# An attention and expert kernel: routing products moved to the ends of pairs, column sums moved into another bank, first loads reordered, weight splits brought forward

## The chip, the core and the metric

The kernel runs on one core of a Trainium2 chip. The metric is the device time of one execution in microseconds (us). The core's engines run side by side, each with an instruction stream in program order, and wait for each other by semaphores: TensorE (PE in the profile; PEld is its weight load), VectorE (DVE), ScalarE (ACT), GpSimd (POOL) and SyncE (SP, which mainly issues DMA). PSUM is the memory that TensorE writes to, in eight banks; SBUF is the other on-chip memory.

## What is computed

Three layers follow each other: an attention with positive random features for 2 x 8 heads of 576 tokens, a mixture of 8 experts with a capacity in token order, and a dense layer with a maximum of three products.

```python
def phi(x):                                   # x scaled by 64 ** -0.25
    h = einsum('bhsd,md->bhsm', x, omega) - sum(x * x, -1, keepdims=True) / 2
    return exp(h - max(h, -1)) / sqrt(128)
kv = einsum('bhsm,bhsd->bhmd', phi(k), v);  z = sum(phi(k), axis=2)
x = einsum('bhsm,bhmd->bhsd', phi(q), kv) / (einsum('bhsm,bhm->bhs', phi(q), z) + 1e-6)
x = x.transpose(0, 2, 1, 3).reshape(1152, 512)
expert = argmax(x @ w_gate, 1);  gate = softmax weight of that expert
# token order: expert e takes its first 288 tokens, the rest give zero rows
y[i] = gate[i] * (relu(x[i] @ w1[expert]) @ w2[expert])
out = maximum(maximum(y @ u1, y @ u2), y @ u3) @ w_out    # 512 -> 768 -> 512
```

## The kernel before

**Attention in pairs.** Two heads make a pair; there are eight, `i` = 0 to 7, four per batch. The main loop stands near the end of the part before the experts. For pair `i` TensorE does `kv_mm` (key features times values, L295, into bank `kb`), `q_t` (transposes of the query features, L328), `z_mm` (column sums of the key features, L308 and L310, into a tile `zq` of the two-bank pool `nb`), `kv_t` (transposed back, L319, into another part of `kb`), `q_th` (the transpose of the last half tile, L333, into `zq`), then for pair `i + 1` the projections (`proj`, L242, and `proj_half`, L264), and last `num(i)` (L342 and L346, into `nb`). VectorE takes a minimum over each projection (`mn`, L249 and L270), ScalarE makes the features with it (`kp` for keys and `qp` for queries, L254 and L274), GpSimd adds the key features up (`ks` and `ksum`, L286 and L288), and VectorE divides what `num` gave (L352 to L369). Projections, transposes and the small tiles of the routing share a pool `pj` of five PSUM banks.

**Routing.** When batch 0's four pairs are done, its routing runs beside pairs 4 to 7 as a generator, `side0`: `route` picks each token's expert (LG to OH), counts tokens per expert with small products `rp` (L456 and L458), chooses the busiest expert, makes a selection matrix `pm` (five 128x288 comparisons, L514) and the tokens' numbers and gates `VAL` (L444 to L450), and gets the row lists from 15 small products `vps` (L529). GpSimd then gathers the rows by DMA (L538) and TensorE transposes them (`tps`, L817) into `xth` and `xtl`. The main loop calls `step()` at fixed places of a pair, and each call takes the generator to its next `yield`; strings such as `YS` and `YP` say where `route` yields. So the program order on every engine is written out by the kernel itself. Batch 1's routing (`side1`) runs the same way beside the first expert's products.

**Experts.** Each pass takes 288 rows through one expert. A float32 product is made of three: operands are split into a rounded part (`hi`, ScalarE, L772) and a rest (`lo`, L773, by GpSimd or VectorE as a letter of `SUBS` says). `pump()` lets `split` take the next weight tile; it may run ahead by `HLB` pairs of buffers. `stage1(0, ...)` (L140 to L142, out of `hps`; eight products, `h1` to `h8` below) begins inside pair 7: three stand before `num(7)`, the others after it. ScalarE takes each out (`hh`, L839) and VectorE forms its rest (`hl`, L840). `stage2` gives `y`. The remaining time is the second expert, a small third job, and the dense layer.

**Loads.** SyncE issues nearly all DMA in program order. The first are omega (`om`, two halves), then pair 0's keys in two parts, its queries, pair 1's, and the values `va`.

Of the kernel before, what the change touches and what calls it, by code (L numbers as in the profile page):

```python
# [8 lines left out]
F32 = mybir.dt.float32  # L9
F32R = mybir.dt.float32r  # L10
BF16 = mybir.dt.bfloat16
# [12 lines left out]
M = 128  # L24
# [11 lines left out]
W1, W2, W3 = 2, 2, 0  # L36
LE, LW = 2, 3
RA, RB, RM = 0, 1, 1
R0, S0, LG1, LV, PMG = 4, 5, 3, (2, 4), ()
# [14 lines left out]
SUBS = "GGGGGGGVVVVVVVVVVVVVVVVVVVVV"  # L54
# [3 lines left out]
YS = "110110011"  # L58
YP = "11000"
LG0, NP0 = 2, 3  # L60
# [6 lines left out]
RAWB, HLB, W64B, EB, CB = 8, 4, 4, 3, 5  # L67

@with_exitstack
def favor_moe_kernel(ctx, tc, qk, va, omt, wg, w1, w2, wm, wo, cap, out):  # L70
# [31 lines left out]
    def load_pair(i):  # L102
        b, p = divmod(i, NP)
        qk_t[i] = ldp.tile([128, 2, 640], F32, tag="qk", name="qk", bufs=2)
        if i == 0:
            SP.dma_start(qk_t[i][:, 0, 0:256], qk[b, p, :, 0, 0:256])
            SP.dma_start(qk_t[i][:, 0, 256:640], qk[b, p, :, 0, 256:640])
            SP.dma_start(qk_t[i][:, 1, :], qk[b, p, :, 1, :])
        else:
            SP.dma_start(qk_t[i], qk[b, p])  # L110
        if i > 1:
            load_va(i)
# [7 lines left out]
    for h in range(2):  # L120
        SP.dma_start(om0[64 * h:64 * h + 64, :], omt[64 * h:64 * h + 64, M * h:M * h + M])
    load_pair(0)

    warm = once.tile([128, 512], BF16, name="warm")
# [4 lines left out]
    for _ in range(WARM):  # L129
        T.matmul(wps, lhsT=warm[:, 128:256], rhs=warm, start=True, stop=True)  # L130
# [101 lines left out]
    KP, QP, QT, KV, KS, MN, ZQ = {}, {}, {}, {}, {}, {}, {}  # L232
# [57 lines left out]
    def kv_mm(i):  # L290

        kb = pk.tile([128, 512], F32, tag="kb", name="kb")
        for t in range(5):
            for h in range(2):
                T.matmul(  # L295
                    kb[64 * h:64 * h + 64, 0:M], lhsT=va_t[i][:, 4 * h + t if t < 4 else 8 + h, :],
                    rhs=KP[i][:, 4 * h + t if t < 4 else 8, :], start=(t == 0), stop=(t == 4),
                    tile_position=(0, 64 * h),
                )
        kvt = kqp.tile([128, M], F32, tag="kvt", name="kvt")  # L300
        copy(KTS[i], kvt, kb[:, 0:M])
        KV[i] = (kb, kvt)

    def z_mm(i):

        ZQ[i] = pn.tile([128, 2, 512], F32, tag="nb", name="zq")
        z = ZQ[i][:, 1, 0:2]
        T.matmul(z, lhsT=KP[i][:, 8], rhs=half, start=True, stop=False)  # L308
        for h in range(2):
            T.matmul(z[:, h:h + 1], lhsT=KS[i][:, h], rhs=one, start=False, stop=(h == 1))  # L310
        kva = kqp.tile([128, 2, VC], F32, tag="kva", name="kva")
        V.tensor_copy(kva[:, :, XC], z)
        KV[i] += (kva,)

    def kv_t(i):

        kb, kvt, kva = KV[i]
        kv = kb[:, 2 * M:2 * M + 2 * XC].rearrange("p (h c) -> p h c", h=2)
        T.matmul(kv, lhsT=kvt, rhs=idw[:, i % NP], start=True, stop=True)  # L319
        copy(KVS[i], kva[:, :, 0:XC], kv)  # L320
        KV[i] = (kb, kva)
# [9 lines left out]
    def q_th(i):  # L331
        ps = ZQ[i][:, 0, 0:128]
        T.transpose(ps, QP[i][:, 8, :], ident)  # L333
        copy(QHS[i], QT[i][:, 8, :], ps)
# [78 lines left out]
    def route(b, lag, slow):  # L413
# [20 lines left out]
        for _ in range(lag):  # L434
            yield
        def gates():
# [86 lines left out]
        for _ in range(LV[b]):  # L523
            yield
# [164 lines left out]
    now = [0]  # L689
    stamp = {}  # L690
# [177 lines left out]
    def step(n=1):  # L868
        for _ in range(n):
# [34 lines left out]
    def side0():  # L904
# [5 lines left out]
        for _ in range(W3):  # L910
            yield
# [42 lines left out]
    def a_step():  # L954
        while len(s1) == 8 and fill:
            step()
# [5 lines left out]
    for i in range(NPR):  # L962
# [7 lines left out]
        step()  # L970
        kv_t(i)
        q_th(i)
# [27 lines left out]
        else:  # L1000
# [3 lines left out]
            a_step()  # L1004
        num(i)
        for _ in range(CP.count(i)):
            next(cons)
        step()
# [322 lines left out]
```

## Time and profile before

| | us |
|---|---|
| three runs | 236.82, 239.42, 241.21 (median 239.42) |
| the profiled execution | 239.82 |
| its span in the trace | 237.7 |

| engine | busy us | share of the span | instructions |
|---|---|---|---|
| PE | 221.4 | 93% | 1924 |
| PEld | 202.8 | 85% | 1924 |
| DVE | 143.1 | 60% | 387 |
| ACT | 109.4 | 46% | 268 |
| POOL | 63.2 | 27% | 94 |

The profile is of one execution. Times count from the start of the span. A row of a timeline gives start, duration, engine, line, operation, output and inputs, and in brackets how long the engine stood idle before and what ended that. Equal neighbours are merged (x16 is sixteen instructions, with one duration from the first to the last). Matmul ends are modelled. PEclk is TensorE's granted clock as a share of its upper level.

### The profile page before, as it was taken

Reading aid. Unit: us, or ns where it says so; the run is one execution under the profiler, and the core shown is the slowest. Engines: PE = TensorE matmul, PEld = TensorE weight load, DVE = VectorE, ACT = ScalarE, POOL = GpSimd, SP = SyncE. Lnnn points to the kernel's source line nnn. Section 1 sums busy time; section 2 is a strip of 40 time slices with the busy share of each in tenths; the row PEclk is TensorE's granted clock in tenths of the full one; section 3 lists DMA queues with packets and bytes.
Section 4 is the critical chain, followed back from the end, with each engine's and each line's share of the span. In section 5 each row is a group of like instructions: output and inputs, shape, how many; then the busy total and the mean of one; then the engine's idle time right before and its main releaser. Section 6 shows DMA issues by size and latency. Waiting matters only on the chain. (4 is left out here: it accounts for less than half of the span.)

```text
span 237.7 us, 5117 instructions
## 1 busy us (share of the span) xinstructions
PE 221.4 (93%) x1924; PEld 202.8 (85%) x1924; DVE 143.1 (60%) x387; ACT 109.4 (46%) x268; POOL 63.2 (27%) x94
## 2 busy tenths in 40 slices
PE   7699999998989999879999999999999999999970
PEld 3598998887967999869899989899999999988870
DVE  0665676798866217997898795675964464432120
ACT  2866966782876443410696936544722213100000
POOL 7004523330486094714100000021321101013120
PEclk9999999997997799979999999999999999999997
DMA  4938759996830812855999678976500000001210
GB/s 118 331 85 280 234 166 338 309 309 228 324 99 3 288 61 81 296 211 165 347 403 411 216 246 276 406 257 219 176 1 3 0 0 3 1 1 47 88 47 29
DMA packets 15821, 42.22 MB, mean 178 GB/s; under 512 B 2269, under 2 KB 5213, under 8 KB 15792
## 3 DMA queue, kind: packets, MB, share of 16 engines
q1 hardware_dynamic: 14304, 39.39, 47.4%
q0 software_dynamic: 800, 2.44, 3.1%
q8 instruction: 17, 0.28, 0.5%
q10 hardware_dynamic: 688, 0.02, 0.2%
q14 instruction: 12, 0.10, 0.1%
HBM read 34.36 MB, written 7.54 MB: 176 GB/s over the span
## 5 line engine op out<-in xcount | busy, mean ns | idle before, releaser
L140 PE MATMUL m<-YH,hi 128*128 128x288 f32 (+1 forms) x144 | 43.6, 303 | 0.0
L141 PE MATMUL m<-YL,hi 128*128 128x288 f32 (+1 forms) x144 | 43.0, 299 | 0.0
L142 PE MATMUL m<-YH,lo 128*128 128x288 f32 (+1 forms) x144 | 42.9, 298 | 0.0
L772 ACT CAST hi<-raw 128x1024 fp32r<-128x1024 f32 x28 | 29.3, 1051 | 26.5 <-PE m L141 16.7
L773 DVE TENSOR_TENSOR lo<-raw,hi 128x1024 fp32r<-128x1024 f32 x21 | 25.9, 1232 | 17.3 <-ACT hi L772 15.9
L140 PEld LDWEIGHTS m<-YH,hi 128*128 128x128 f32 x144 | 27.1, 188 | 0.8 <-issue 0.6
L254 ACT ACTIVATE kp<-ps,mn 128x128 f32<-128x128 f32 x64 | 17.4, 383 | 21.1 <-DVE mn L249 21.1
L142 PEld LDWEIGHTS m<-YH,lo 128*128 128x128 f32 x144 | 27.1, 188 | 0.0
L141 PEld LDWEIGHTS m<-YL,hi 128*128 128x128 f32 x144 | 27.1, 188 | 0.0
L249 DVE TENSOR_REDUCE mn<-ps 128x4 f32<-128x512 f32 x32 | 20.5, 683 | 7.1 <-PE ps L242 7.1
L672 ACT CAST e<-w 128x512 f16<-128x512 bf16 x24 | 18.8, 785 | 10.2 <-DMA w<-in_wm_dram 6.8
L140 PE MATMUL y<-hh,hi 128*128 128x288 f32 x64 | 20.4, 318 | 0.8 <-DVE KC L476 0.8
L286 POOL TENSOR_TENSOR ks<-kp 128x512 f32<-128x512 f32 x7 | 9.1, 1298 | 42.4 <-ACT kp L254 42.4
L1160 POOL TENSOR_TENSOR H2L<-mxt,H2H 128x288 fp32r<-128x288 f32 (+1 forms) x10 | 9.5, 948 | 38.7 <-ACT H2H L95 24.9
L242 PE MATMUL ps<-om,qk 64*128 64x128 f32 x256 | 18.7, 300 | 0.9 <-DMA qk<-in_qk_dram 0.9
L141 PE MATMUL y<-hl,hi 128*128 128x288 f32 x64 | 19.5, 305 | 0.0
L142 PE MATMUL y<-hh,lo 128*128 128x288 f32 x64 | 19.5, 305 | 0.0
L242 PEld LDWEIGHTS ps<-om,qk 64*128 64x128 f32 x256 | 17.0, 209 | 2.9 <-DVE om L919 1.1
L773 POOL TENSOR_TENSOR lo<-raw,hi 128x1024 fp32r<-128x1024 f32 x7 | 16.5, 2380 | 10.9 <-ACT hi L772 10.7
L140 PE MATMUL hps<-xth,hi 128*128 128x288 f32 x64 | 19.3, 301 | 0.0
L141 PE MATMUL hps<-xtl,hi 128*128 128x288 f32 x64 | 18.9, 295 | 0.0
L142 PE MATMUL hps<-xth,lo 128*128 128x288 f32 x64 | 18.8, 294 | 0.0
(228 smaller groups left out, 466.8 us busy)
## 6 DMA issues: line engine op xcount, KB each, us to landing
w<-in_wm_dram SPq DMA_DIRECT2D x18, 512.0 KB, 5.5
raw<-in_w_dram SPq DMA_DIRECT2D x16, 512.0 KB, 6.1
qk<-in_qk_dram SPq DMA_DIRECT2D x7, 640.0 KB, 5.5
craw<-in_w_dram SPq DMA_DIRECT2D x8, 512.0 KB, 9.3
w<-in_wo_dram SPq DMA_DIRECT2D x6, 512.0 KB, 5.2
va<-in_va_dram SPq DMA_DIRECT2D x8, 320.0 KB, 5.8
out_dram<-zt SPq DMA_DIRECT2D x9, 256.0 KB, 5.4
XD<-X SPq DMA_DIRECT2D x2, 960.0 KB, 6.3
```

What stands on the lines that cost most here:

```text
L140: T.matmul(ps, lhsT=wh, rhs=xh, start=start, stop=False)
L141: T.matmul(ps, lhsT=wh, rhs=xl, start=False, stop=False)
L142: T.matmul(ps, lhsT=wl, rhs=xh, start=False, stop=stop)
L242: T.matmul(ps[h][:, t, :], lhsT=qk_t[i][r, s, 128 * t:128 * t + 128], rhs=om[r], start=True, stop=True, tile_position=(64 * h, 0),)
L249: V.tensor_reduce(MN[i][:, k:k + 4], PJ[i, s][h], axis=AX.X, op=ALU.min)
L254: A.activation(dst[:, 4 * h + t, :], PJ[i, s][h][:, t, :], AF.Exp, bias=mn[:, k + t:k + t + 1], scale=-1.0)
L286: eng.tensor_tensor(u, k4[:, 0:2], k4[:, 2:4], ALU.add)
L672: A.copy(e.bitcast(F16).rearrange("p (c two) -> p c two", two=2)[:, :, 1], src.bitcast(BF16)[:, 4:4 * WH + 4:4])
L772: A.copy(hi, raw)
L773: (G if SUBS[n] == "G" else V).tensor_tensor(lo, raw, hi, ALU.subtract)
L1160: engine(HLS[k]).tensor_tensor(H2L[:, fc, n0:n1], mv, H2H[:, fc, n0:n1], ALU.subtract)
```

## The change

Seven things change.

- `z_mm` writes its sums into the bank `kb`, next to `kv_t`'s output, and `q_th` into the second quarter of that bank; `zq` goes. One VectorE copy then takes values and sums together (`kva`, 128x146), and the separate 128x2 copy goes. `q_th` is issued ahead of `kv_t`.
- A flag `spot` is true in the `step` at a pair's end. `rp`, `vps` and the row transposes of batch 0 wait for it, so they follow `num` (pairs 4, 5 and 6). The yields `YS`, `YP`, `LG0`, `LV`, `W1` to `W3` are set anew.
- The first load on SyncE is now the first part of the keys; omega's halves go one by ScalarE's queue and one as SyncE's second load.
- `HLB` goes from 4 to 6: six pairs of split buffers.
- Ahead of `num(7)` three more `pump()` calls split three more weight tiles.
- `SUBS`: the rests of tiles 4 to 6 are formed by VectorE, not GpSimd.
- The warm-up tile shrinks from 512 to 128 columns, read four times over; `kvt` has one buffer.

```diff
-W1, W2, W3 = 2, 2, 0
+W1, W2 = 2, 1
-R0, S0, LG1, LV, PMG = 4, 5, 3, (2, 4), ()
+R0, S0, LG1, LV, PMG = 4, 5, 3, (0, 4), ()
-SUBS = "GGGGGGGVVVVVVVVVVVVVVVVVVVVV"
+SUBS = "GGGGVVVVVVVVVVVVVVVVVVVVVVVV"
-YS = "110110011"
-YP = "11000"
-LG0, NP0 = 2, 3
+YS = "111100101"
+YP = "01000"
+LG0, NP0 = 0, 3
-RAWB, HLB, W64B, EB, CB = 8, 4, 4, 3, 5
+RAWB, HLB, W64B, EB, CB = 8, 6, 4, 3, 5
@@ load_pair, i == 0
             SP.dma_start(qk_t[i][:, 0, 0:256], qk[b, p, :, 0, 0:256])
+            SP.dma_start(om0[64:128, :], omt[64:128, M:2 * M])
             SP.dma_start(qk_t[i][:, 0, 256:640], qk[b, p, :, 0, 256:640])
@@
-    for h in range(2):
-        SP.dma_start(om0[64 * h:64 * h + 64, :], omt[64 * h:64 * h + 64, M * h:M * h + M])
+    A.dma_start(om0[0:64, :], omt[0:64, 0:M])
     load_pair(0)
-    warm = once.tile([128, 512], BF16, name="warm")
+    warm = once.tile([128, 128], BF16, name="warm")
-        T.matmul(wps, lhsT=warm[:, 128:256], rhs=warm, start=True, stop=True)
+        T.matmul(wps, lhsT=warm, rhs=warm.unsqueeze(1).to_broadcast([128, 4, 128]), start=True, stop=True)
@@ z_mm, kv_t, q_th
-        ZQ[i] = pn.tile([128, 2, 512], F32, tag="nb", name="zq")
-        z = ZQ[i][:, 1, 0:2]
+        kb, kvt = KV[i]
+        z = kb[:, 2 * M:2 * M + 2 * VC].rearrange("p (h c) -> p h c", h=2)[:, :, XC]
...
+        T.matmul(kv[:, :, 0:XC], lhsT=kvt, rhs=idw[:, i % NP], start=True, stop=True)
+        copy(QHS[i], QT[i][:, 8, :], kb[:, M:2 * M])
         kva = kqp.tile([128, 2, VC], F32, tag="kva", name="kva")
-        V.tensor_copy(kva[:, :, XC], z)
...
+        copy(KVS[i], kva, kv)
-        ps = ZQ[i][:, 0, 0:128]
-        T.transpose(ps, QP[i][:, 8, :], ident)
-        copy(QHS[i], QT[i][:, 8, :], ps)
+        T.transpose(KV[i][0][:, M:2 * M], QP[i][:, 8, :], ident)
@@ route, twice: before rp and before vps
+        while slow and not spot[0]:
+            yield
@@ step
-    def step(n=1):
-        for _ in range(n):
+    def step(end=False):
+        spot[0] = end
@@ side0, before the row transposes
-        for _ in range(W3):
+        while not spot[0]:
             yield
@@ main loop
+        q_th(i)
         kv_t(i)
-        q_th(i)
...
+        if not more:
+            for _ in range(3):
+                pump()
         num(i)
         for _ in range(CP.count(i)):
             next(cons)
-        step()
+        step(True)
```

Line numbers in the rows of the changed program below are its own, a few off those of before: its L339 and L343 are `num`, L530 is `vps`, L513 `pm`, L842 `hl`, L775 the rest `lo`.

TensorE's queue in pair 5, before, from the last projection (`psh`) to pair 6's first product (`kb`):

```order
L264 MATMUL psh<-om,qk 64x128 x4
L529 LDWEIGHTS pm
L529 MATMUL vps<-VAL,pm 128x6
...
L342 MATMUL nb<-kva,qt 128x73 x8
L346 MATMUL nb<-kva,qt 64x73 x2
L295 MATMUL kb<-kp,va 64x128 x10
```

The same place in the changed program:

```order
L264 MATMUL psh<-om,qk 64x128 x4
L339 MATMUL nb<-kva,qt 128x73 x8
L343 MATMUL nb<-kva,qt 64x73 x2
L530 LDWEIGHTS pm
L530 MATMUL vps<-VAL,pm 128x6
...
L295 MATMUL kb<-kp,va 64x128 x10
```

`vps`, fifteen loads and products that need all five `pm`, moved from ahead of `num` to behind it; nothing of pair 6 may pass it.

VectorE's queue in the same pair, before, from the selection's start to the first minimum reduction of pair 6's projections (`sm` are small routing tiles, `KC` a count):

```order
L510 SCALAR_TENSOR_TENSOR sm_903<-sm_903,RG 128x5
L446 TENSOR_TENSOR sm_859<-GT,VAL 128x5
L514 TENSOR_SCALAR pm<-io,sm_903 128x288
L448 CAST VAL<-sm_859 128x5
L312 COPY kva<-zq 128x2
L514 TENSOR_SCALAR pm<-io,sm_903 128x288
L450 TENSOR_TENSOR VAL<-sm_859,VAL 128x5
L95 COPY kva<-kb 128x2x72
L95 COPY qt<-zq 128x128
L514 TENSOR_SCALAR pm<-io,sm_903 128x288 x3
L519 COPY KC<-KT 128x8
L249 TENSOR_REDUCE mn<-ps_956 128x4
```

In the changed program, from the first reduction on:

```order
L249 TENSOR_REDUCE mn<-ps_923 128x4
L249 TENSOR_REDUCE mn<-ps_924 128x4
L270 TENSOR_REDUCE mn<-psh 128x2
L249 TENSOR_REDUCE mn<-ps_933 128x4
L249 TENSOR_REDUCE mn<-ps_934 128x4
L509 SCALAR_TENSOR_TENSOR sm_955<-sm_955,RG 128x5
L445 TENSOR_TENSOR sm_880<-GT,VAL 128x5
L513 TENSOR_SCALAR pm<-io,sm_955 128x288
L447 CAST VAL<-sm_880 128x5
L513 TENSOR_SCALAR pm<-io,sm_955 128x288
L449 TENSOR_TENSOR VAL<-sm_880,VAL 128x5
L513 TENSOR_SCALAR pm<-io,sm_955 128x288 x3
```

The selection moved from ahead of the five reductions to behind them.

VectorE's queue around `num(7)`, before, from the rests of `h1` and `h2` to the division:

```order
L840 SCALAR_TENSOR_TENSOR hl<-hps,hh 128x288 x2
L352 TENSOR_SCALAR dn_149<-nb 128x2x4
L353 TENSOR_SCALAR dn_149<-nb 64x2
L354 RECIPROCAL dn_149<-dn_149 128x10
L357 TENSOR_TENSOR X<-nb,dn_149 128x2x4x64
```

And in the changed program:

```order
L842 SCALAR_TENSOR_TENSOR hl<-hps,hh 128x288 x2
L775 TENSOR_TENSOR lo<-raw,hi 128x1024 x3
L349 TENSOR_SCALAR dn_149<-nb 128x2x4
L350 TENSOR_SCALAR dn_149<-nb 64x2
L351 RECIPROCAL dn_149<-dn_149 128x10
```

Three splits moved in ahead of the division; one more (the tile after them) now stands between the rests of `h3` and `h4`, ahead of the second routing's counts, and GpSimd has two splits fewer behind pair 7.

## Rows read from the trace of the kernel before

**Rows 1.** Stretches: width, busy us (instructions) of each engine, PEclk, DMA share, GB/s

```profile
18.26:26.42 8.16, 8.16 (x101) 7.38 (x101) 5.36 (x17) 5.89 (x23) 3.06 (x10) 1.00 0.69 236
...
42.81:52.08 9.27, 8.50 (x108) 7.60 (x108) 7.97 (x28) 6.86 (x27) 2.71 (x3) 1.00 0.98 323
...
52.08:63.70 11.62, 10.64 (x116) 9.52 (x116) 9.59 (x48) 6.58 (x25) 2.43 (x4) 0.85 0.81 303
...
63.70:77.08 13.38, 12.13 (x113) 9.60 (x111) 8.72 (x30) 9.38 (x28) 10.17 (x8) 0.88 0.20 60
...
77.08:81.97 4.89, 4.89 (x39) 4.44 (x38) 0.96 (x3) 2.02 (x5) 0.00 (x0) 0.64 0.81 244
...
86.84:104.06 17.22, 14.69 (x128) 14.07 (x126) 13.22 (x51) 4.98 (x10) 9.21 (x5) 1.00 0.52 177
...
104.06:112.06 8.00, 8.00 (x52) 8.00 (x50) 6.98 (x32) 1.05 (x1) 3.50 (x4) 0.79 0.42 143
...
112.06:230.00 117.94, 117.94 (x919) 111.17 (x918) 70.05 (x130) 47.02 (x76) 15.76 (x17) 1.00 0.44 161
```

**Rows 2.** What TensorE waited for, whole span: us in total, times, longest

```profile
PE kb L295 <- DMA va<-in_va_dram: 1.4, 1, 1.4
...
PE zq L308 <- DVE sm L503: 0.8, 1, 0.8
...
PE y L140 <- DVE KC L476: 0.8, 1, 0.8
```

**Rows 3.** Timeline of TensorE, three places

```profile
21.61 2.06 PE L242 MATMUL ps<-om,qk 64*128 64x128 f32 x32
...
103.53 0.60 PE L529 MATMUL vps<-VAL,pm 128*128 128x6 bf16 x15 [1.75 <-DVE hl L840]
...
116.90 1.10 PE L817 MATMUL tps<-ident,rows 128*128 128x128 f32 x6
```

**Rows 4.** Timeline of SyncE's DMA issues, the start

```profile
0.80 1.21 SPq L121 DMA_DIRECT2D om<-in_omt_dram  x2
...
3.16 0.43 SPq L108 DMA_DIRECT2D qk<-in_qk_dram  x1
```

**Rows 5.** DMA issues: engine, count, KB each, median us from issue to landing

```profile
qk<-in_qk_dram SPq DMA_DIRECT2D x1, 320.0 KB, 3.7
...
rows<-XD,IX POOLq DMA_INDIRECT x6, 3.4
```

**Rows 6.** Timeline of VectorE: an ordinary pair, then the second routing

```profile
21.72 0.29 DVE L95 COPY qt<-zq 128x128 f32<-128x128 f32 x1
...
24.64 1.28 DVE L249 TENSOR_REDUCE mn<-ps 128x4 f32<-128x512 f32 x2
...
89.17 0.17 DVE L352 TENSOR_SCALAR dn<-nb 128x8 f32<-128x8 f32 x1 [2.83 <-PE nb L346]
...
95.21 1.72 DVE L473 TENSOR_TENSOR sm<-TOT,KT 128x8 f32<-128x8 f32 x1
...
100.02 0.15 DVE L399 TENSOR_REDUCE sm<-sm 128x1 f32<-128x8 f32 x1
...
101.28 0.16 DVE L510 SCALAR_TENSOR_TENSOR sm<-sm,RG 128x5 f32<-128x5 f32 x1
...
103.02 1.55 DVE L840 SCALAR_TENSOR_TENSOR hl<-hps,hh 128x288 fp32r<-128x288 f32 x4
```

**Rows 7.** Timeline of GpSimd: an ordinary pair, then the second routing

```profile
25.79 1.30 POOL L286 TENSOR_TENSOR ks<-kp 128x512 f32<-128x512 f32 x1 [4.95 <-ACT kp L254]
...
27.17 0.72 POOL L288 TENSOR_TENSOR ksum<-ks 128x256 f32<-128x256 f32 x1
...
94.50 4.76 POOL L773 TENSOR_TENSOR lo<-raw,hi 128x1024 fp32r<-128x1024 f32 x2 [3.20 <-ACT hi L772]
...
108.26 1.25 POOL L538 DMA_INDIRECT rows<-XD,IX  x1 [0.30 <-issue]
```

**Rows 8.** Costliest groups of the page: count | busy us, mean ns | idle before

```profile
L773 DVE TENSOR_TENSOR lo<-raw,hi 128x1024 fp32r<-128x1024 f32 x21 | 25.9, 1232 | 17.3 <-ACT hi L772 15.9
```

## What the change does to the time: the prediction

> **What bounds the kernel now.** I read it by stages first: the table of busy time by stretch [rows 1], cut at TensorE's own marks. From 112.06 us to 230 us TensorE is busy 117.94 of 117.94 us at full clock, so nothing outside TensorE's own work is to be won there. An ordinary attention pair takes 8.16 us and is full as well. The loss sits between: pair 4 takes 9.27 us, pair 5 11.62, pair 6 13.38; pair 7 needs 4.89 to the first expert product; and the stretch from pair 7's `num` (86.84) to the end of `vps` (104.06) holds 14.69 us of work in 17.22. So whatever the change wins, apart from the start, has to come from about 55 us in the middle.
>
> Second comes the granted clock in the same rows, whose two levels are 1.2 and 2.4 GHz: 0.85, 0.88, 0.64 and 0.79 in four stretches. A mean of 0.85 over 11.62 us is 2 x 0.15 x 11.62 = 3.5 us at the lower level, which costs half of that, 1.7 us; the others work out to 1.6, 1.8 and 1.7. Before them TensorE waited: 0.8 us in pair 5 for a VectorE operation of the routing, at `z_mm` [rows 2], and 1.75 us before `vps` [rows 3]. Third are the waits by line [rows 2] and the timelines of VectorE and GpSimd [rows 6, 7], which say what was late.
>
> **The change part by part**, against the profiled execution's 239.8 us (span 237.7; the shown median is 239.4, so the two stand level).
>
> *Start.* SyncE issued two loads of omega in 1.21 us before the keys, and the queries' half, issued at 3.16, landed 3.7 us later [rows 4, 5], at 6.86, with `va` later still: TensorE waited 1.4 us for it [rows 2]. One omega load now goes by ScalarE's queue, so SyncE's later loads, `va` too, move up by 0.6 us. Omega's second half is still SyncE's second load, so TensorE's first product stays where it is; what follows moves up. I take -0.6; nothing if ScalarE were the limit, -0.8 at most with the smaller warm-up tile. Only the issue slots are counted, not more bandwidth.
>
> *Sums in the values' bank.* `z_mm` no longer takes the `nb` tile, so it doesn't wait for `num`'s readers; one small VectorE copy per pair goes, hidden in idle time. But `z` now waits for ScalarE's copy `kvt`, which reads that bank and stands behind the features. An ordinary pair has little room there; bounds 0 and +0.1 a pair; I take +0.3 for eight.
>
> *Routing products at the ends, pair 4.* `rp` stands behind `num` and no longer waits for a feature buffer, and `z`'s wait goes too. The pair falls to 8.16 plus a few small products, 8.3: -1.0.
>
> *Pair 5*, where a new wait arises. Its seven late selection rows (`far`, `VAL`, five `pm`) stood ahead of the five minimum reductions in VectorE's queue; now they stand behind them, and `vps` follows `num`. From the pair's first product: VectorE's two copies end at 21.72 + 0.29 - 18.26 = 3.75; twelve routing operations take 100.02 to 101.28, 1.26 us [rows 6], so the reductions start at 5.0 and, two pairs of 1.28 [rows 6] and a short one between, some 2.9 in all, end at 7.9. The selection takes 101.28 to 103.02, 1.74: the last `pm` is done at 9.6 and `vps` at 10.0. `num` alone would be through at 8.2, so TensorE stands about 1.3 us, with all of pair 6 queued behind it. That is the bound if GpSimd doesn't interfere. The other bound: GpSimd's key sums, 1.30 and 0.72 us [rows 7], start just then, once the keys' features are out; if the small copies and differences between the `pm` are held until each ends, 1.5 us more: 11.5. I take 10.7, between, since such small operations are the kind held in [rows 6], but the `pm` themselves have no row beside a GpSimd operation. Against 11.62: -0.9.
>
> The lock is in this trace: a 128x8 difference took 1.72 us at 95.21, while GpSimd's splits ran from 94.50 to 99.26 [rows 6, 7]. The Trainium skill (SBUF — State Buffer, "Who interferes with whom") says that a VectorE operation with two SBUF inputs and a GpSimd one that reads SBUF exclude each other for the whole instruction, the first to issue winning; the trace agrees. By that rule alone pair 5 would take 11.5 us, and it speaks against this order.
>
> *Pairs 6 and 7.* They took 13.38 + 4.89 = 18.27, of which 3.4 us went to the lower clock. The work is 8.16, twelve row transposes (six took 1.10 [rows 3], so 2.2), and 21.61 - 18.26 = 3.35 from a pair's first product to its projections, where pair 7 has the expert products instead: 13.7. The gathered rows may arrive up to 0.4 late, since `vps` and the list after it come later. After a stand of over a microsecond in pair 5 I expect one stretch at the lower clock again, 1.7 us, which hides the rows: 15.4, so -2.85. If the clock stays up: 14.1, -4.2. If it falls for as long as before: 17.1, -1.2.
>
> *Stage 1.* GpSimd keeps two splits fewer after `num`, so two operations of the second routing are free: the difference that took 1.72 us, and the limit behind it, held until the split ended at 99.26 [rows 6, 7], together some 4 us. That removes the waits of 0.8 (`y`) [rows 2] and 1.75 (`vps`) [rows 3]. In exchange three splits of 1.23 us each [rows 8] stand on VectorE ahead of `num(7)`'s division. VectorE was idle 2.83 us there [rows 6]; 3 x 1.23, plus about 0.7 in which the first is held by GpSimd's last split of 2.38 us, is 4.4, so the division and all routing behind it start 1.6 later. `rp` then waits about 0.6, the next two expert products 0.9 and 0.5 (the seventh split stands between their two `hl`): 2.0 come, 2.5 go, about -0.6. Afterwards the gather decides: before, its third part was issued at 108.26 [rows 7] and took 3.4 [rows 5], to 111.7, against the transposes at 112.06. Even at full clock these can move up only by what `vps` moved, plus 0.4. I take -0.9 (bounds 0 and -1.4). Six buffers only allow the forward splits; the later splits run two ahead of a TensorE that never waited there.
>
> Sum: -0.6 + 0.3 - 1.0 - 0.9 - 2.85 - 0.9 = -5.95, from 239.8 to **233.9 us**, 2.3% under the median. About 2% (4.8 us) is what a measurement of this kernel can tell from no change, so this stands at 234.6's edge.
>
> **The rivals.**
> - *Clean middle, 231.9.* Nothing holds the `pm` (pair 5 at 10.0: a further -0.7) and the clock stays up through pairs 6 and 7 (a further -1.35), rest as above. For it: TensorE stood 1.4 us at the start [rows 2] and no low clock followed. Against it: each middle wait of 0.8 us or more was followed by a low stretch.
> - *GpSimd's lock in pair 5, 237.3.* The `pm` chain is held by both key sums (11.5: +0.8), the longer stand pulls the clock down for as long as it was low before in pairs 6 and 7 (17.1: +1.65), and stage 1, whose gather waits for the same queue, gives nothing (+0.9). For it: [rows 6], and that all three hang on VectorE's longer queue. The page's rule on the shared port is this rival's first term.
> - *Slower, 245.* The seventh load of expert weights, queued on SyncE behind pair 6's store of `X`, lands late. ScalarE's cast of it stands ahead of the routing's exponential, and VectorE's split of it ahead of `num(7)`. Before, that cast came only after this exponential, so lateness was covered; now every microsecond beyond about 10 us after pair 7's start is one of TensorE's. From 6 us late the total is above the old one; 11 us give 245. Against it: the 320 KB load landed in 3.7 us [rows 5], and no row of the expert loads shows a wait of TensorE.
> - *Not what it says*: the rows move, but the clock falls in the same places whatever the waits. Then only the waits go: -0.6 + 0.3 - 1.0 - 1.2 - 0.6, 236.7; counted with the second rival.
>
> **How the numbers follow.** Forecast 233.9 (232.5 to 235.6): 0.42. Clean, 230 to 232.5: 0.25. Lock or low clock anyway, 235.6 to 238.5: 0.27. Slower: 0.06. The range, 230.3 to 238.0, leaves out the slower rival and the outer ends of the two others, some 0.15 in all. Faster by over 2% (under 234.6): the clean case and two thirds of the forecast, 0.53. Within 2%: 0.41. Slower by over 2%: 0.06.
>
> **What would show it.** Right: pair 5's `vps` waits for a `pm` by 1 to 3 us; pairs 4 and 6 show no wait for a feature buffer; the difference of totals in the second routing takes 0.2 us, not 1.7; VectorE's first forward split takes about 1.9 us beside GpSimd's. Wrong: if pair 5 shows no wait at `vps`, my queue count failed; if granted clock stays 1.00 in pairs 5 to 7 after such a wait, the 1.7 is not owed; if the products after `rp` don't wait, the forward splits cost nothing.

## The result and the profile after

The changed kernel takes 236.07 us (median of 20 executions, 234.17 to 238.35), where the kernel before, run in turn with it, takes 241.12. The ratio is 0.9883, with a 95% interval from 0.9848 to 0.9919. It leaves out executions over 1.5% above the fastest of each kernel (the rest average 238.6 and 235.9), so it is nearer to 1 than the two medians are. The change is a gain of 1.2%; I had forecast 2.3% to 2.5%. The direction was right, and 236.07 lies inside the range, but the gain is half of the forecast.

The profiled execution took 235.41 us with a span of 233.7, against 239.82 and 237.7: 4.0 us less, where my sum said 5.95. The profiled execution of the kernel before thus lies 1.2 us above the average just given, that of the changed kernel 0.4 below its own. The table of busy time by stretch, cut at TensorE's marks as [rows 1] was, shows where they went (columns: stretch and width, then busy us of TensorE, its weight load, VectorE, ScalarE, GpSimd, the granted clock, DMA share, GB/s):

```profile
18.53:42.78 24.25, 24.25 (x295) 22.10 (x295) 15.10 (x44) 17.61 (x65) 9.52 (x32) 1.00 0.80 258
42.78:51.23 8.45, 8.45 (x106) 7.60 (x104) 6.84 (x23) 6.46 (x25) 2.29 (x3) 1.00 0.99 332
51.23:63.09 11.86, 9.29 (x117) 8.18 (x113) 10.68 (x49) 7.60 (x28) 3.34 (x4) 0.91 0.58 213
63.09:74.51 11.42, 11.42 (x107) 10.08 (x104) 6.49 (x25) 7.30 (x21) 8.50 (x6) 0.80 0.47 169
74.51:78.65 4.14, 4.14 (x44) 3.55 (x44) 2.73 (x9) 3.21 (x11) 1.31 (x2) 1.00 0.63 200
78.65:100.07 21.42, 19.75 (x164) 19.01 (x162) 16.62 (x60) 8.75 (x16) 6.16 (x3) 1.00 0.55 178
100.07:106.53 6.46, 6.46 (x51) 6.46 (x49) 5.94 (x31) 2.11 (x2) 3.36 (x4) 1.00 0.70 233
...
106.53:112.82 6.29, 5.95 (x48) 4.88 (x47) 2.98 (x8) 3.30 (x7) 0.12 (x1) 1.00 0.84 291
112.82:126.86 14.04, 13.20 (x96) 12.93 (x97) 13.97 (x24) 11.36 (x21) 0.82 (x1) 1.00 0.96 375
```

The last two, from the first row transposes to the second expert's first product and from there to its first `y`, have these counterparts in the kernel before, which the prediction had not looked at one by one:

```profile
112.06:117.93 5.87, 5.87 (x48) 4.85 (x47) 3.93 (x10) 3.10 (x5) 0.93 (x1) 1.00 0.92 338
117.93:130.83 12.90, 12.90 (x97) 12.90 (x97) 11.88 (x20) 10.17 (x19) 0.00 (x0) 1.00 1.02 406
```

| stretch | before, us | after, us | difference | forecast |
|---|---|---|---|---|
| to the end of pair 0's `num` | 18.26 | 18.53 | +0.27 | -0.6 |
| pairs 1 to 3 | 24.55 | 24.25 | -0.30 | about +0.1 |
| pair 4 | 9.27 | 8.45 | -0.82 | -1.0 |
| pair 5 | 11.62 | 11.86 | +0.24 | -0.9 |
| pairs 6 and 7, to the first expert product | 18.27 | 15.56 | -2.71 | -2.85 |
| to the end of the second `vps` | 22.09 | 21.42 | -0.67 | with the next row |
| to the first row transposes | 8.00 | 6.46 | -1.54 | -0.9 for the two |
| to the second expert's first `y` | 18.77 | 20.33 | +1.56 | 0 |
| from there | 106.87 | 106.84 | -0.03 | 0 |
| sum | 237.7 | 233.7 | -4.0 | -5.95 |

(The bank's +0.3 was spread over eight pairs in the forecast; 0.2 of it has no line of its own.)

The largest difference, -2.71, can't be put down to the change. The low granted clock of the kernel before in pairs 6 and 7 (0.88 and 0.64 in [rows 1]) belongs to its one profiled execution. The run `before_new_loads`, reported below, differs from the kernel before only in its first loads, and its two stretches from pair 6 to the first expert product are at full clock:

```profile
63.67:75.57 11.90, 10.93 (x113) 8.89 (x113) 7.61 (x26) 9.35 (x28) 10.03 (x8) 1.00 0.24 69
75.57:78.81 3.24, 3.24 (x38) 2.96 (x38) 1.74 (x7) 1.91 (x5) 0.00 (x0) 1.00 0.46 172
```

That is 15.14 us instead of 18.27, with the same operations in the same order there. Against it the changed kernel's 15.56 is no gain. The whole span of that run was 234.3, only 0.6 above the changed kernel's. The averages differ by 2.7 us, between this 0.6 and the 4.0 of the two profiles; that would fit if some executions of the kernel before have the low stretch and others don't, but in how many was not counted.

What TensorE waited for (us in total, times, longest), to be held against [rows 2]:

```profile
PE vps L530 <- DVE VAL L449: 2.3, 1, 2.3
PE kb L295 <- DMA va<-in_va_dram: 2.0, 1, 2.0
PE hps L140 <- DVE hl L842: 1.1, 2, 0.9
...
PE hps L141 <- DVE xtl L811: 0.8, 1, 0.8
PE rp L455 <- DVE OH L424: 0.6, 1, 0.6
```

Gone are the waits at `zq` and `y`, and those for the feature buffers. Of these the kernel before had one of 0.5 at `rp` and two at the row transposes:

```profile
PE tps L817 <- ACT kp L254: 1.0, 2, 0.5
```

Three things stand in their place: `vps` of pair 5 (2.3), `rp` and two `hps` in stage 1 (1.7 together), and two `hps` of the second expert (0.3 and 0.8), which no step of mine had (the wait of 0.3 is for `idt`, a small VectorE tile). The timelines show the first. VectorE in pair 5, then GpSimd, then TensorE:

```profile
56.35 1.28 DVE L249 TENSOR_REDUCE mn<-ps 128x4 f32<-128x512 f32 x2
...
59.32 0.37 DVE L513 TENSOR_SCALAR pm<-io,sm 128x288 bf16<-128x288 f32 x1
59.61 1.24 DVE L447 CAST VAL<-sm 128x5 bf16<-128x5 f32 x1
60.75 0.35 DVE L513 TENSOR_SCALAR pm<-io,sm 128x288 bf16<-128x288 f32 x1
61.03 0.69 DVE L449 TENSOR_TENSOR VAL<-sm,VAL 128x5 bf16<-128x5 f32 x1
61.63 0.92 DVE L513 TENSOR_SCALAR pm<-io,sm 128x288 bf16<-128x288 f32 x3
```

```profile
59.44 1.37 POOL L286 TENSOR_TENSOR ks<-kp 128x512 f32<-128x512 f32 x1 [6.97 <-ACT kp L254]
60.89 0.80 POOL L288 TENSOR_TENSOR ksum<-ks 128x256 f32<-128x256 f32 x1
```

```profile
61.78 1.38 PE L530 MATMUL vps<-VAL,pm 128*128 128x6 bf16 x15 [2.33 <-DVE VAL L449]
63.09 2.40 PE L295 MATMUL kb<-kp,va 128*64 128x128 f32 x20
```

The cast ends with GpSimd's `ks` (60.8), the difference with its `ksum` (61.7). In the second routing, with GpSimd idle, the same two take 0.17 us each, so 1.6 us are held. Then `kv_mm`, 1.31 us in other pairs, takes 2.40, at the lower clock (0.80 over pair 6).

### The profile page after: what moved, and what is told of

Same layout as the page of the kernel before. It is cut to its first block, busy times and chain, and to the rows that moved or that the text cites. A ratio compares the mean times of both kernels' runs of the same rounds, so it can differ in the third digit from the quotient of the medians.

```text
span 233.7 us, 5130 instructions
## 1 busy us (share of the span) xinstructions
PE 217.4 (93%) x1924; PEld 199.8 (86%) x1924; DVE 141.8 (61%) x382; ACT 109.7 (47%) x268; POOL 56.1 (24%) x91
## 5 line engine op out<-in xcount | busy, mean ns | idle before, releaser
L775 DVE TENSOR_TENSOR lo<-raw,hi 128x1024 fp32r<-128x1024 f32 x24 | 30.1, 1262 | 15.2 <-ACT hi L774 15.2
L673 ACT CAST e<-w 128x512 f16<-128x512 bf16 x24 | 18.8, 785 | 11.7 <-DMA w<-in_wm_dram 10.6
L140 PE MATMUL y<-hh,hi 128*128 128x288 f32 x64 | 19.6, 306 | 0.0
L677 DVE SCALAR_TENSOR_TENSOR raw<-w,e 128x512 int32<-128x512 int32 x24 | 17.1, 714 | 3.5 <-ACT e L673 3.4
L142 PE MATMUL y<-hh,lo 128*128 128x288 f32 x64 | 18.8, 294 | 0.0
L141 PE MATMUL y<-hl,hi 128*128 128x288 f32 x64 | 18.8, 294 | 0.0
L1163 DVE TENSOR_TENSOR mxt<-m,mxt 128x288 f32<-128x288 f32 (+1 forms) x24 | 11.1, 462 | 12.1 <-PE m L142 11.6
L242 PEld LDWEIGHTS ps<-om,qk 64*128 64x128 f32 x256 | 15.7, 195 | 2.7 <-DVE om L922 1.4
```

What stands on the lines that cost most here:

```text
L140: T.matmul(ps, lhsT=wh, rhs=xh, start=start, stop=False)
L141: T.matmul(ps, lhsT=wh, rhs=xl, start=False, stop=False)
L142: T.matmul(ps, lhsT=wl, rhs=xh, start=False, stop=stop)
L242: T.matmul(ps[h][:, t, :], lhsT=qk_t[i][r, s, 128 * t:128 * t + 128], rhs=om[r], start=True, stop=True, tile_position=(64 * h, 0),)
L673: A.copy(e.bitcast(F16).rearrange("p (c two) -> p c two", two=2)[:, :, 1], src.bitcast(BF16)[:, 4:4 * WH + 4:4])
L677: V.scalar_tensor_tensor(dst.bitcast(I32), src[:, 1:2 * WH + 1:2], 13, e, ALU.logical_shift_right, ALU.bitwise_or)
```

## The experiments

The kernels were measured in four groups, each with the kernel before in it, whose median was 238.3 to 241.2. A ratio is to the kernel before of the same group, so ratios of different groups compare only roughly; mechanisms are held against rows, which are of one execution each.

**Gates ahead of the reductions.** The gates are three small operations that make `VAL` (L445 to L449): a difference, a cast and a difference.

```
+        if slow:
+            for _ in gt:
+                pass
         if slow and YS[8] == "1":
             yield
         V.scalar_tensor_tensor(far, far, BIG, r, ALU.mult, ALU.add)
-        next(gt)
+        next(gt, None)
```

> The changed kernel, with the three small gate operations (a difference, a cast and a difference into VAL) moved ahead of the five minimum reductions in pair 5; the five pm stay behind them. In the changed kernel the cast took 1.24 us and the last difference 0.69 beside GpSimd's key sums, where the second routing's took 0.17 each, so 1.6 us are held. Theory (GpSimd's lock on these two is what turns a short wait into 2.33 us): the two take 0.2 each again, vps waits 0.3 to 0.8 us, and TensorE's granted clock stays at 1.00 behind it (pair 6 in 10.5 or less instead of 11.42): 2.5 to 3.3 us less in all. Rival 1 (the queue is too long by itself, the pm are then held in their stead): vps still waits 1.8 or more, no gain. Rival 2 (the wait goes, but the clock falls at that place whatever the wait): the wait shrinks, pair 6 still shows a low stretch, 1.3 to 1.8 us less.

Ratio 0.9919 (0.9876 to 0.9962). The cast and the last difference took 0.18 us each again, but pair 5 took 12.14 us, not less, and TensorE stood 2.5 us at `vps` in three pieces. VectorE's rows show why; the first is of all five `pm`, the others of the second and the third:

```profile
59.55 3.05 DVE L516 TENSOR_SCALAR pm<-io,sm 128x288 bf16<-128x288 f32 x5
...
59.84 1.40 DVE L516 TENSOR_SCALAR pm<-io,sm 128x288 bf16<-128x288 f32 x1
...
61.17 0.88 DVE L516 TENSOR_SCALAR pm<-io,sm 128x288 bf16<-128x288 f32 x1
```

The five `pm` take 3.05 us instead of 1.5. The first starts just ahead of GpSimd's sums (59.68) and takes its usual 0.37 us. The second takes 1.40 and the third 0.88; they end just after GpSimd's `ks` (61.08) and `ksum` (61.87). Rival 1 held: whatever stands at that place is held, the `pm` too. My prediction had left open whether the `pm` are of that kind.

**GpSimd's sums after the `pm`.** This takes the overlap away and leaves VectorE's order as it is.

```
+    PMS = []
...
+        PMS.append(pm)
...
-            sums(nx)
+            if nx != 6:
+                sums(nx)
...
             step()
             step()
+            if nx == 6:
+                G.tensor_copy(sm([128, 1]), PMS[0][:, NT - 1, 0:1])
+                sums(nx)
```

> The changed kernel; GpSimd's key sums for pair 6 are issued in pair 5 only when the fifth pm is out (one 128x1 copy of it on GpSimd ahead of them), the order on VectorE stays. In the run with the gates first, the five pm took 3.05 us beside those sums where five unheld ones take 1.5, so what stands there is held, whatever it is. Theory (GpSimd's lock is about half of the wait, the queue the other half): the cast and the difference take 0.2 each, the wait at vps falls from 2.33 to 0.7 to 1.2 us, the first pair-6 product comes about 10.2 to 10.6 us after pair 5's (11.86 before), and z_mm(6) doesn't wait for the later sums. If a wait of about 1 us is still followed by a lower clock, pair 6 keeps its 10.6 to 11.4; if not, 9.7. Total 1.2 to 3 less. Rival (something else holds VectorE there): the two operations stay at 1.2 and 0.7, no gain.

Ratio 0.9662 (0.9606 to 0.9719), the lowest of all; span 231.2. VectorE, and the stretches of pairs 5 and 6:

```profile
60.24 0.17 DVE L448 CAST VAL<-sm 128x5 bf16<-128x5 f32 x1
60.31 0.36 DVE L514 TENSOR_SCALAR pm<-io,sm 128x288 bf16<-128x288 f32 x1
60.59 0.17 DVE L450 TENSOR_TENSOR VAL<-sm,VAL 128x5 bf16<-128x5 f32 x1
```

```profile
51.99:62.21 10.22, 9.23 (x114) 8.09 (x116) 9.06 (x47) 7.14 (x27) 1.62 (x4) 1.00 0.49 181
62.21:71.66 9.45, 9.45 (x105) 8.13 (x107) 6.56 (x25) 7.52 (x22) 7.75 (x7) 1.00 0.74 278
```

The theory held. The wait at `vps` fell from 2.33 to 0.7, pair 5 from 11.86 to 10.22, and pair 6 ran at full clock in 9.45 instead of 11.42. The overlap with GpSimd was worth 1.6 us by itself and 1.2 to 2.0 more through the clock behind it: pair 6 took 11.42 in the changed kernel, but 10.63 to 10.85 in three variants of it that kept the stand (gates first, old loads, old splits). Pair 7's `z_mm` now waits 0.4 us for its own `ksum`, which GpSimd begins at 74.69, behind two splits and its `ks`; pair 6's later sums were done at 63.9 and nothing waited for them.

**Selection ahead of the reductions**, as it stood before.

```
-YS = "111100101"
-YP = "01000"
+YS = "111100100"
+YP = "00000"
```

> The changed kernel, with the whole selection (limit rows, gates and five pm) ahead of the five minimum reductions in pair 5, as it stood before the change, vps still behind num. Theory (VectorE's queue order decides pair 5): no wait at vps, but the reductions start about 1.8 us later and the features with them, so kv_mm(6) waits 1.2 to 2 us for ScalarE's last key feature; pair 5 to the end of vps in about 8.9 instead of 11.86, pair 6 longer by the wait; total 0.5 to 2 us less, depending on the clock after the shorter wait. Rival (the reductions have slack, nothing waits): total 3 us or more less. Rival (the wait only moves and the clock falls as before): within 0.5 us of the changed kernel.

Ratio 0.9861 (0.9763 to 0.9959), span 231.2.

```profile
51.87:61.57 9.70, 8.75 (x116) 7.96 (x112) 8.37 (x45) 4.55 (x17) 1.19 (x2) 1.00 0.51 193
61.57:71.98 10.41, 10.41 (x106) 8.33 (x104) 7.26 (x29) 10.07 (x33) 8.52 (x7) 1.00 0.70 255
```

TensorE stood 0.95 us at `vps`, now for ScalarE's key feature, and the query transposes of pair 6 took 2.14 us instead of 1.09, as each waits for its feature. The theory had the place nearly right (two waits instead of one at `kv_mm`). It had the gain (0.5 to 2 us) somewhat small by the span, which fell by 2.5; the ratio's interval can't tell. The clock stayed up: GpSimd starts its sums behind the whole selection, and nothing is held. So the queue by itself costs 2.0 us in this order, and 1.5 in the one above (0.7 at `vps`, and `vps` itself 1.34 us instead of 0.60, as it follows the last `pm`).

**The load order**, undone in the changed kernel and done alone in the kernel before.

```
-            SP.dma_start(om0[64:128, :], omt[64:128, M:2 * M])
...
-    A.dma_start(om0[0:64, :], omt[0:64, 0:M])
+    for h in range(2):
+        SP.dma_start(om0[64 * h:64 * h + 64, :], omt[64 * h:64 * h + 64, M * h:M * h + M])
```

> The changed kernel with the load order of before (both omega halves on SyncE ahead of the keys). In the changed kernel the first pair's num ended at 18.53 where before it ended at 18.26, and the wait for va was 1.98 us instead of 1.39, against my forecast of 0.6 less. Theory A (the new order makes va land later, because more transfers share the queues at once): with the old order num ends at 18.2 to 18.3 again and the total is 0.2 to 0.4 us less. Theory B (va's landing varies from run to run, the order itself is worth what the issue slots say): num ends later than 18.5, va lands 0.3 to 0.6 later, total 0.3 to 0.6 more.

> The kernel before with the new load order alone (omega's first half on ScalarE's queue, its second half behind the keys' first piece). Theory A (the new order delays va): va's wait 1.9 to 2.1 us instead of 1.39, first num ends at 18.5 instead of 18.26, total 0.2 to 0.4 us more. Theory B (issue slots decide): va lands 0.6 earlier, first num ends at 17.7 to 18.0, total 0.3 to 0.6 less.

Ratios 0.9946 (0.9897 to 0.9995) and 0.9995 (0.9931 to 1.0059). `kv_mm` of pair 0 starts at 10.55 us with the old order in the changed kernel and 10.47 with the new one, at 10.16 with the new order in the kernel before and 10.03 with the old. Neither theory fits: the order is worth nothing either way. The first line is a wait of TensorE in the changed kernel with the old loads; the rows of SyncE and ScalarE are of the changed kernel:

```profile
PE kb L295 <- ACT qp L254: 1.9, 1, 1.9
```

```profile
3.50 1.27 SPq L117 DMA_DIRECT2D va<-in_va_dram  x2
...
9.37 0.42 ACT L274 ACTIVATE kp<-psh,mn 128x128 f32<-128x128 f32 x1
```

`va` was issued at 3.50 instead of 4.24. But ScalarE's last key feature ends at 9.79 us where it ended at 9.52, and `kv_mm`, which needs both, starts at 10.47 with `va` named as what ended its wait (2.0 us, above), where it started at 10.03 before. Of these four runs three name `va` and one ScalarE, so which of the two limits the start isn't settled.

**The two attention parts alone**, each put into the kernel before: the sums in the values' bank, and the routing products at the ends of pairs (their diffs are those of the change).

> The kernel before with the sums in the values' bank alone (z and the half transpose into kb, one copy of 146 columns on VectorE). Forecast in my sum: a little dearer, 0 to +0.1 a pair. The changed kernel showed 8.06 us a pair against 8.17, so I now expect 0.1 less a pair, and the waits of z_mm (0.8 in pair 5, 0.3, 0.2) gone: 0.8 + 1.3 = 2 us less if the clock in pair 5 then stays up or falls as before; pair 5 in 10.7 or less instead of 11.62. Rival (the 0.8 in pair 5 only moves to num, which needs the same routing operations out of VectorE's way): pair 5 as before, 0.7 less in all.

> The kernel before with the routing products placed at the ends of pairs and nothing else (z still in the nb bank). Theory: pair 4 falls from 9.27 to about 8.7 (rp's wait for a feature buffer goes, z's stays), pair 5 is no better (11.9 to 12.6, vps waits for VAL as in the changed kernel, z waits too), pairs 6 and 7 to the first expert product fall from 18.27 to 15.5 to 16.5, as the six row transposes no longer wait in the middle of a pair; total 1.5 to 3 less. Rival (the placement gives nothing by itself, its gain came with the bank of z): within 0.7 of before.

Ratios 0.9843 (0.9755 to 0.9931) and 0.9829 (0.9761 to 0.9898): by these each alone wins more than the whole change did in its own comparison (0.9883). That can't be taken for their worth: six of the seven executions of the kernel before in this group showed a mean granted clock of 0.958 to 0.964, as its profiled one did (0.964), where that with the new loads showed 0.979. The first three rows are of the bank alone (pairs 1 to 3, pair 5, pair 6), the last two of the placement alone (pairs 5 and 6):

```profile
18.74:42.99 24.25, 24.25 (x295) 22.10 (x295) 15.10 (x44) 17.61 (x65) 9.52 (x32) 1.00 0.79 255
51.73:63.13 11.40, 9.39 (x115) 8.63 (x115) 10.36 (x50) 7.30 (x27) 2.89 (x4) 0.92 0.78 305
63.13:75.41 12.28, 11.32 (x113) 9.58 (x112) 6.78 (x21) 8.80 (x26) 9.82 (x7) 0.93 0.21 74
```

```profile
52.12:64.04 11.92, 9.39 (x116) 8.17 (x112) 10.72 (x49) 7.57 (x28) 3.38 (x4) 1.00 0.58 209
64.04:75.06 11.02, 11.02 (x107) 9.59 (x104) 6.61 (x26) 6.91 (x20) 8.06 (x6) 0.85 0.52 183
```

The bank takes 0.1 us off an ordinary pair (24.55 to 24.25 over three) and removes the 0.8 at `z_mm`; but pair 5 keeps 11.40, since `vps`, then still ahead of `num`, waits 2.0 us for a feature. That was the rival. The placement gives pair 5 the same 11.9 us with a wait of 2.3 as in the changed kernel, so the new wait belongs to it. Pairs 6 and 7 take 15.34 with the placement alone and 15.34 with the bank alone, and 15.14 with the new loads alone, where neither part is in. So neither part is shown to win anything there, and what each is worth by itself stays open.

**The splits.** Undone in the changed kernel (`SUBS`, `HLB = 4`, no forward pumps), and done alone in the kernel before.

> The changed kernel with the splits of before (seven on GpSimd, four buffers, no forward splits). In the changed kernel the way from pair 7's first expert product to the end of the second vps took 21.42 us, with waits of 0.57 at rp, 0.88 and 0.22 at two hps; before it took 22.09, with 0.8 at y and 1.75 at vps. Theory (my sum: the forward splits cost about 2 and save about 2.5): the three waits go, the held difference of 1.7 us and limit of 2.4 come back, waits of 0.8 and 1.7 at y and vps; 22.0 to 22.2, total 0.6 more. Rival (the routing before was late only because all of it was late, so here the old splits cost nothing): 20.0 to 20.5 us, total about 1 less.

> The kernel before with its splits alone changed (four on GpSimd, six buffers, three forward splits). Theory: the held difference and limit in the second routing fall from 1.7 and 2.4 us to 0.2, the waits at y (0.8) and vps (1.75) go, 1.7 us of new waits at rp and two hps come, so 22.1 becomes 21.4; without the wait of 1.75 the clock behind vps stays at 1.00, 8.0 becomes 6.45; and the second expert's first products wait 1.1 to 1.5 for the row split. Net 0.7 + 1.5 - 1.3 = 0.9 less than before. Rival (the clock falls there all the same): 8.0 stays, 0.3 more to 0.7 less.

Ratios 0.9802 (0.9743 to 0.9861) and 0.9951 (0.9848 to 1.0054). The old splits in the changed kernel, from pair 7's first expert product to the second `vps`, to the row transposes, to the second expert's first product and to its first `y`:

```profile
77.75:99.86 22.11, 19.57 (x165) 18.96 (x163) 14.65 (x55) 8.62 (x16) 13.16 (x6) 1.00 0.56 192
99.86:107.84 7.98, 7.98 (x51) 7.98 (x49) 6.97 (x32) 1.04 (x1) 3.44 (x4) 0.79 0.50 150
107.84:113.72 5.88, 5.88 (x49) 4.86 (x47) 3.93 (x10) 3.10 (x5) 0.93 (x1) 1.00 0.93 357
113.72:126.62 12.90, 12.90 (x98) 12.90 (x98) 11.88 (x20) 10.48 (x19) 0.00 (x0) 1.00 1.02 392
```

That is 48.87 us, against 48.21 in the changed kernel: the splits win 2.2 us up to the transposes (the held operations and the lower clock behind `vps`) and lose 1.55 behind them. The whole span was 0.5 us shorter all the same (233.2), as pairs 6 and 7 took 15.0 us, with a granted clock of 0.84 instead of 0.80 in pair 6. In the kernel before, with the new splits alone, the first two stretches took 21.30 and 6.44, but the last took 15.35 instead of 12.90, with a granted clock of 0.89 in it, and no gain is left.

**Six buffers or forward splits?** Both on the kernel with the sums after the `pm`: `HLB = 4` in the one, no forward pumps in the other.

> The kernel with the key sums after the pm (231.2 us of span in its profile), with four weight buffers instead of six; the three forward splits then become one ahead of num(7)'s division, and every later split stands one place later in ScalarE's and VectorE's queues. In that kernel, as in the changed one, rp waited 0.5 us, two hps 0.9 and 0.2, and the first products of the second expert 0.8 for a row split, behind a cast on ScalarE that waited 2.4 us for its weights (in the changed kernel). Theory (six buffers pull a split of weights that have not landed ahead of the row copies): with four buffers the late waits of 0.8 and 0.3 go, from the second expert's first product to its first y 12.9 instead of 14.0; the waits at rp and hps shrink too, as two splits fewer stand ahead of the division: 1.1 to 2.5 less in all. Rival (the loads are late for every order, DMA is full there): the late waits stay, total within 0.5 or up to 1 less from rp alone.

> The kernel with the key sums after the pm, without the three forward pumps ahead of num(7), six buffers kept: one split stands ahead of the division, the others come behind the later hl, the order from the row copies on is that of the changed kernel. Theory: the waits at rp (0.5) and at the first hps behind it (0.9) go or fall under 0.3 together, the way from pair 7's first expert product to the second vps falls from 21.3 to 20 to 20.5; the late waits of 0.8 and 0.3 in the second expert stay, since the casts still run two ahead there; total 0.5 to 1.3 less. Rival (the forward splits were hidden; without them the first y waits for its split): no gain or 0.5 more.

Ratios 0.9769 (0.9706 to 0.9832) and 0.9791 (0.9716 to 0.9867), spans 231.0 and 232.1. Four buffers, then no forward splits, over the same four stretches as above:

```profile
76.99:96.10 19.11, 19.02 (x154) 18.48 (x152) 13.87 (x56) 8.43 (x15) 6.18 (x3) 1.00 0.52 181
96.10:102.99 6.89, 6.89 (x64) 6.85 (x62) 6.41 (x32) 1.05 (x1) 3.45 (x4) 1.00 0.67 238
102.99:110.03 7.04, 6.16 (x48) 4.87 (x46) 5.67 (x13) 3.16 (x5) 0.94 (x1) 1.00 0.73 246
110.03:122.94 12.91, 12.91 (x98) 12.91 (x97) 11.88 (x21) 9.50 (x17) 0.00 (x0) 1.00 1.02 396
```

```profile
76.67:97.02 20.35, 19.60 (x165) 18.95 (x163) 15.11 (x57) 7.97 (x15) 6.19 (x3) 1.00 0.56 196
...
103.48:111.47 7.99, 6.23 (x48) 4.88 (x47) 4.27 (x12) 2.77 (x5) 0.45 (x3) 1.00 0.75 266
111.47:125.52 14.05, 13.21 (x97) 12.94 (x98) 13.98 (x24) 11.64 (x22) 0.82 (x1) 1.00 0.99 376
```

With six buffers the last stretch keeps its 14.05 and its wait of 0.8, forward splits or not; with four it is 12.91 and nothing waits. So the buffers are the cause. What stands in the way is on ScalarE; the rows are of the changed kernel:

```profile
109.89 1.05 ACT L774 CAST hi<-raw 128x1024 fp32r<-128x1024 f32 x1 [2.37 <-DMA raw<-in_w_dram]
110.84 0.39 ACT L95 CAST xth<-tps 128x288 fp32r<-128x288 f32 x1
```

A cast that runs one weight further ahead waits 2.37 us for weights still on their way, and the copy of the rows, whose transposes were done at 109.7, is issued behind it. VectorE's splits and row splits follow late, and TensorE with them.

The forward splits' own price is the other theory's: without them the first stretch falls by 0.96 us. But then the transposes wait 1.3 us for the gathered rows, and the gain is not kept. With four buffers the second `vps` stands a few products earlier, so its first two stretches are read together: 26.0 us against 27.8 with six. Over all four they win 1.67 us (47.62 to 45.95), in the range of the theory. But the spans of the kernels with six and with four buffers are level (231.2 and 231.0), as the rival for the total said: 0.8 us is lost ahead of pair 5, where the two don't differ, and 0.7 behind the four stretches, where waits of 0.8 and 0.3 stand against one of 0.5. Why these come was not looked into. Both kernels are faster than the changed one: all eight executions of the two (232.10 to 233.38) lie below the lowest of its twenty (234.17).

## Why the prediction was half right

**The start (-0.6 forecast, +0.3 measured).** The step that failed is "what follows moves up". I counted issue slots, and the slots did move up by 0.7; but `kv_mm` started at 10.47 us, not earlier than before (10.03). ScalarE's features ended no earlier (9.79 against 9.52), which I had named as the bound at nothing and not taken, and `va`, though issued earlier, was what ended TensorE's wait. Why it didn't land earlier is open. Undoing and doing the loads alone agree on about zero. The smaller part of the 0.9 may be scatter: pair 0 begins anywhere from 9.6 to 10.6 us over the runs.

**The bank (+0.3 forecast for eight pairs, -0.1 a pair measured).** I had expected `z` to wait for ScalarE's copy. It doesn't. The bank alone shows the 0.1; what saves it was not looked into.

**Pair 4 (-1.0, measured -0.82).** Right, with its mechanism.

**Pair 5 (-0.9, measured +0.24).** Mechanism right, size wrong, and by the table the largest miss: 1.1 of the 2 us that were missing. The new wait at `vps` came where I had put it, with the queue that I had counted: the reductions start 5.1 us into the pair (5.0 forecast) and end at 7.9 (7.9). The term that failed is "I take 10.7, between". Between an end without and one with GpSimd's lock I took the middle, when [rows 6] already showed the lock; `vps` ended at 11.86. Taking the overlap away gave 10.22, near my free bound of 10.0. The Trainium skill (SBUF — State Buffer, "Who interferes with whom") lists casts and operations with a scalar among those that can take the port that GpSimd shares. The runs agree: beside GpSimd's sums a cast took 1.24 us instead of 0.17, and five `pm` 3.05 instead of 1.5.

**Pairs 6 and 7 (-2.85, measured -2.71).** The changed kernel's side was right: one stretch at the lower clock behind the stand at `vps`, 15.56 us against 15.4. The side of before was not, and that the difference came out near is luck. The step that failed is "They took 13.38 + 4.89 = 18.27, of which 3.4 us went to the lower clock": I counted this loss as the kernel's own, to be won back, when one profile showed it. With the same order `before_new_loads` took 15.14. Both executions had the two waits of 0.5 and 0.4 us for feature buffers shortly ahead of the place (the one before also 0.3 earlier in pair 6), so I took the clock of one execution for an effect of the order. With 15.14 in place of 18.27 the same reasoning gives +0.3 here instead of -2.85. This is the largest error of the sum, and the table hides it, since the measured difference has it too. What held the clock down in one execution and not in the other is open.

That the changed kernel's own low stretch is owed to the stand is borne out by the runs, one profiled execution each. After a stand of 2.3 to 2.5 us at this place, pair 6 showed a granted clock of 0.80 to 0.86 in all five kernels that had one; after 0.7 to 0.95 us it showed 1.00 in all four. A second execution can differ here too: the kernel with four buffers had a mean granted clock of 0.995 in its profiled execution and 0.975 to 0.976 in its three others, in nearly the same time. Without the lock my clean rival's middle came out: pair 5 to pair 7's first expert product in 24.4 us, where I had 10.0 + 14.1.

**Stage 1 (-0.9, measured -0.65).** The sum was near and its parts were not. Right: the difference of totals took 0.16 us instead of 1.72, the three splits held `num(7)`'s division until 87.73, `rp` and two `hps` waited 0.6, 0.9 and 0.2 (I had 0.6, 0.9 and 0.5). Missed on one side: the lower clock behind the old `vps` wait, 1.54 us, which I let be used up by the gather. (Four kernels with that wait showed this stretch; in the bank alone it was absent, see the end.) Missed on the other: 1.56 us in the second expert. The sentence that failed is that six buffers "only allow the forward splits" and that later splits run ahead of "a TensorE that never waited there". I looked at who waits for a split, and not at what is queued behind it on ScalarE while it waits for its own load. The gather as the next limit was no error of mechanism: without forward splits it did hold the transposes, for 1.3 us.

Of the rivals, the one with GpSimd's lock gave pair 5 its size (11.86 against 11.5). By time the median of 236.07 lies in that rival's band (235.6 to 238.5), the profiled execution's 235.41 at the upper end of the forecast's. But the rival's two other terms didn't come: pairs 6 and 7 took 15.56 us and not 17.1, and stage 1 won something. The late seventh load never came. The signs that I had named came as well: a wait of 2.3 us at `vps` in pair 5 (for `VAL`, not a `pm`), none for a feature buffer in pairs 4 and 6, 2.02 us for the first forward split.

## What to carry to other kernels

When a row shows an operation held by another engine and the change puts more operations of that kind beside it, price them as held, not half-held, and look first whether the other engine can start later: here one dependency on GpSimd was worth about as much as the whole change. More buffers are not free where one queue serves two purposes: ask what stands behind each early operation on its engine if its input is late. A stand of TensorE can cost more than its length, so count the stretch behind it. But don't take a low-clock stretch in one profile for the kernel's own: look first whether a second execution of the same order has it.

## What the hardware showed that I had not expected

- Who starts first decides, by a tenth of a microsecond: the `pm` that began 0.13 us ahead of GpSimd's `ks` took its usual 0.37 us, the one queued behind it 1.40, and the cast that began 0.17 us behind `ks` in the changed kernel 1.24.
- The lower clock is not a matter of the stand's length alone. Behind the second `vps`, a stand of 1.75 to 1.8 us was followed by 0.79 in four kernels and by 1.00 in a fifth (the bank alone); stands of up to 2.0 us for the first values were followed by 1.00 each time. In pair 5 a wait of 0.84 us at `z_mm` was followed by 0.85 in the kernel before and with the new loads alone, and one of 0.85 by 1.00 with the new splits alone. And pairs 6 and 7 of the same order showed 0.88 and 0.64 in one execution, 1.00 and 1.00 in another. What tells these apart was not tried.
